# First batch's scores from float32 q and k as loaded, and an earlier, denser weight conversion, in an attention and feed-forward kernel

## The chip, the cores and the metric

The kernel runs on one core of a Trainium2 chip. The metric is the device time of one execution in microseconds (us); lower is better. PE is the matmul engine, DVE the vector engine, ACT the scalar engine, POOL GpSimd, and SP the engine whose queue issues nearly all transfers here.

## What is computed

Talking-heads attention over 4 batches, 12 heads, 448 positions and head size 64, followed by a feed-forward block of 1792 tokens, 768 to 2048 to 768. The weights of the feed-forward block arrive as float64.

```
def _attn_ref(q, k, v, w_pre, w_post):
    scores = np.matmul(q, k.transpose(0, 1, 3, 2)) / np.sqrt(64)
    scores = np.einsum('bhij,hg->bgij', scores, w_pre)
    scores = scores - np.max(scores, axis=-1, keepdims=True)
    attn = np.exp(scores)
    attn = attn / (np.sum(attn, axis=-1, keepdims=True) + 1e-09)
    attn = np.einsum('bhij,hg->bgij', attn, w_post)
    return np.matmul(attn, v)

def _moe_ref(x, w_in, w_out):
    h = x @ w_in
    g = h * (1.0 / (1.0 + np.exp(-1.702 * h)))
    return g @ w_out
```

## The kernel before

**Precision.** Most products run in float16 with each operand split into an upper and a lower half (three products for one). For that, the size of a tensor is found first (`squares`, L122: sums of squares on ACT and DVE; `join`, L136: a product with ones on PE), then a power of two as its scale (`scale`, L139), then the upper half (`upper_part`, L177, on ACT or POOL) and the lower half (`lower_part`, L186, on DVE). The mix with `w_pre` is a float32 product, which PE carries out as two matmul records.

**Attention.** A batch's 448 query rows are cut in 4 chunks of 120 (the last of 88). For each chunk and each of 6 pairs of heads `scores` (L210) makes the products of q and k in two PSUM banks; the two heads of a pair use the two halves of the partitions. `keep_scores` (L227) copies them to SBUF (3 buffers), and `send_scores` (L234) writes them to memory, from where `gather` (L242) reads them back with the rows of 10 queries times 12 heads on the partitions. Each such group is a step; there are 45 a batch and 180 in all. A step's work: `mix` (L252, PE), `peak` (L261, DVE), `expo` (L267, ACT, then a small operation on POOL), `inverse` (L279, DVE: the reciprocal that ends a step), `weigh`, `upper` and `lower` (L283 to L297, POOL and ACT), three steps later `post` (L305, PE), then `keep_upper` on ACT and `keep_lower` on DVE. When a chunk's steps are done, `context` (L337) multiplies with v.

**Weights.** `convert` (L401) turns one slice of one weight matrix (8 slices of w_in, 8 of w_out) from float64 to two float16 halves. A slice has 3 parts. Each part is fetched on SP's queue (L414, 512 KB, 3 buffers), passes through five DVE steps (`magnitude`, `least`, `shift`, `rest`, `sign`, L421 to L441) and a sum of squares on ACT. After the join and the scale each part gets its upper half (`w_upper`, L467, ACT) and its lower half (`w_lower`, L470, DVE), and the slice is stored (L476) in memory. `fetch_w` (L506) loads a converted slice (`wt`) for a unit, that is for one slice and one batch.

**Feed-forward.** A unit's work is cut in 12 quanta of six products: `hidden` (L510, products h at L520) and `project` (L553, products po at L559).

**What sets the order.** Instructions stand in the order in which the Python code issues them. The main loop runs over the steps i. A list of jobs with a first step, an engine, a cost and predecessors is worked off by `run_jobs` (L631) with tokens that `refill` (L601) gives each engine per step. A conversion's jobs get their first step from the call of `convert` (L688): 2, 8, 14 and so on, two matrices a slice, so 12 steps a slice. Once a batch's x is ready (`x_done`), each step may do 2.15 quanta; a unit's quantum is done only if its `wt` load was issued, and `fetch_ahead` (L725) issues the load only when the slice's store was issued at least a step before. What is left after the last step is done densely. Ahead of the loop stand the loads of k and q, their sizes and splits, the first chunk's scores, its first four gathers, and the size of v.

Of the kernel before, what the change touches and what calls it, by code (L numbers as in the profile page):

```python
# [9 lines left out]
F32 = mybir.dt.float32  # L10
# [3 lines left out]
AF = mybir.ActivationFunctionType  # L14
# [24 lines left out]
def attention_then_feed_forward(ctx, tc, q, k, v, w_pre, w_post, w_in, w_out, out):  # L39
# [76 lines left out]
    def load(name, b, i, use, tag="op"):  # L116

        t = st[name, b, i] = flow.tile(SH[name], F32, name=f"{name}{use}{i}_{b}", tag=tag, bufs=THIRDS)
        w = t.shape[1]
        nc.sync.dma_start(out=t, in_=SRC[name][b][:, i * w:(i + 1) * w])  # L120

    def squares(name, b, i, eng, n=1):  # L122
        t = st[name, b, i]
        if ("m" + name, b) not in st:
            st["m" + name, b] = stat.tile([t.shape[0], THIRDS * n], F32, name=f"m{name}_{b}", tag="m" + name)
        x = t.rearrange("p a b -> p (a b)")
        w = x.shape[1] // n
        for y in range(n):
            m = st["m" + name, b][:, i * n + y:i * n + y + 1]
            square_sum(x[:, y * w:(y + 1) * w], m, eng[y % len(eng)])  # L130
# [5 lines left out]
    def join(name, b):  # L136
        add_all(top_of(name, b), st["m" + name, b])

    def scale(name, b):  # L139

        m = top_of(name, b)
        e = stat.tile([128, 1], F32, name=f"e{name}_{b}", tag="e" + name)
        s = stat.tile([128, 1], F32, name=f"s_{name}{b}", tag="s" + name)
        root_bits(e, m)
        nc.vector.reciprocal(s, e)
        nc.vector.tensor_scalar_mul(s, s, 2.0 ** -50)
        nc.vector.tensor_scalar_mul(e, e, 2.0 ** 63)
        st["e" + name, b], st["s" + name, b] = e, s
        if name == "v":
            nc.vector.tensor_scalar(  # L150
                ex[:, b:b + 1], e, e_wp, 2.0 ** -12, op0=ALU.mult, op1=ALU.mult
            )

    def mixing(b):
        c = stat.tile([128, 1], F32, name=f"c_{b}", tag="c")
        nc.vector.tensor_tensor(c, st["eq", b], st["ek", b], op=ALU.mult)
        wa = keep.tile([KG, KG], F32, name=f"wa_{b}", tag="wa", bufs=2)
        nc.vector.tensor_scalar(
            wa, w_mix.rearrange("p i g -> p (i g)"), c[:KG, 0:1], 0.125 * 2.0 ** -26,
            op0=ALU.mult, op1=ALU.mult,  # L160
        )
        st["wa", b] = wa
# [14 lines left out]
    def upper_part(name, b, i, eng):  # L177
        u, _, src, s = pair_of(name, b, i)
        if eng == "A":
            nc.scalar.activation(u, src, AF.Copy, scale=s)  # L180
        elif eng == "D":
            nc.vector.tensor_scalar(u, src, s, 1.0, op0=ALU.mult, op1=ALU.mult)
        else:
            nc.gpsimd.tensor_scalar(u, src, s, 1.0, op0=ALU.mult, op1=ALU.mult)

    def lower_part(name, b, i, eng="D"):  # L186
        u, l, src, s = pair_of(name, b, i)
        nc.vector.scalar_tensor_tensor(l, src, s, u, op0=ALU.mult, op1=ALU.subtract)
# [21 lines left out]
    def scores(b, c, pr, tag=("gen", 3)):  # L210

        i0, n = chunk(b, c)
        two = [bank(f"qk_{b}_{c}_{pr}_{x}", *tag) for x in range(2)]
        done = open_banks[-2:] if tag[0] == "gen" else []
        w = NPAIR // THIRDS
        qp, kp = st["qp", b, pr // w], st["kp", b, pr // w]
        terms = ((0, 0), (0, 1), (1, 0))
        for t, (i, j) in enumerate(terms):
            for x in range(2):
                rs = slice(x * D, (x + 1) * D)  # L220
                nc.tensor.matmul(  # L221
                    two[x][:n, :S], qp[rs, i, pr % w, i0:i0 + n], kp[rs, j, pr % w, :],
                    start=t == 0, stop=t == len(terms) - 1,
                )
        return two, done

    def keep_scores(b, c, pr, two, engs):  # L227
        i0, n = chunk(b, c)
        t = flow.tile([CI, 2, S], F32, name=f"sc_{b}_{c}_{pr}", tag="sc", bufs=3)
        for x in range(2):  # L230
            (nc.scalar.copy if engs[x] == "A" else nc.vector.tensor_copy)(t[:n, x, :], two[x][:n, :S])  # L231
        return t

    def send_scores(b, c, pr, t):  # L234
        n = chunk(b, c)[1]
        nc.sync.dma_start(out=sd[b, c][:, 2 * pr:2 * pr + 2, :], in_=t[:n])
# [164 lines left out]
    def convert(kind, s, first):  # L401
# [5 lines left out]
        def part(a):  # L407
            return slice(a * HW, (a + 1) * HW)
# [52 lines left out]
                    ew[:, s, 2:3], ew[:, s, 0:1], e, 2.0 ** -20, op0=ALU.mult, op1=ALU.mult  # L461
                )

        def w_upper(a):
            if a == 0:
                t["p"] = flow.tile([128, 2, WN], F16, name=f"{nm}_p", tag="wc", bufs=1)
            nc.scalar.activation(t["p"][:, 0, part(a)], t["f", a].bitcast(F32), AF.Copy, scale=t["s"])  # L467

        def w_lower(a):
            nc.vector.scalar_tensor_tensor(  # L470
# [21 lines left out]
        j = job(first, "D", 0.9, scale_w, after=[(j, 0)])  # L492
        low = []
        for a in range(NP):
            up = job(first, "A", 0.65, lambda a=a: w_upper(a), after=[(j, 1)] + [(x, 0) for x in stores[-1:]])
            low.append(job(first, "D", 0.7, lambda a=a: w_lower(a), after=[(up, 1)]))
        parts.extend(low)
        stores.append(job(first, None, 0, store, after=[(x, 1) for x in low]))
# [126 lines left out]
    def job(first, eng, cost, f, after=(), stage=None, urgent=False):  # L625
        j = {"urgent": urgent, "first": first, "eng": eng, "cost": cost, "f": f, "stage": stage,
             "after": [a if isinstance(a, tuple) else (a, 1) for a in after]}
        jobs.append(j)
        return j
# [55 lines left out]
    conv_done = {}  # L685
    for s in range(NS):
        for kind in range(2):
            conv_done[kind, s] = convert(kind, s, 2 + (s * 2 + kind) * 6)  # L688


    quanta = []
# [52 lines left out]


    for i in range(THIRDS):
        load("k", 0, i, "a")
    for i, w in enumerate((w_pre, w_post)):
        nc.scalar.dma_start(out=wrep[:, i, :], in_=w.unsqueeze(0).to_broadcast([GI, H, H]))
    nc.scalar.dma_start(out=wall, in_=w_post.unsqueeze(0).to_broadcast([128, H, H]))  # L750
    nc.vector.memset(ones, 1.0)
    last_pp.append(ps.tile([128, 512], F32, name="sums", tag="av", bufs=1))
    for i in range(THIRDS):
        load("q", 0, i, "a", "w64")
    nc.vector.memset(tops, 0.0)
    nc.scalar.activation(warm, tops[:, 0:1], AF.Exp)
    nc.gpsimd.memset(sel, 1.0)
# [5 lines left out]
        out=sel, in_=sel, pattern=[[H, GI]], compare_op=ALU.is_ge, fill=0.0,  # L763
        base=H - 1, channel_multiplier=-1,
    )
    for name in "kq":
        for i in range(THIRDS):
            squares(name, 0, i, "AD", 2)
        join(name, 0)
        scale(name, 0)  # L770
        for i in range(THIRDS):
            upper_part(name, 0, i, "AGA"[i])
        if name == "k":
            nc.vector.tensor_tensor(
                w_mix,
                wrep[:, 0, :].unsqueeze(1).to_broadcast([KG, GI, H]),
                sel.unsqueeze(2).to_broadcast([KG, GI, H]),
                op=ALU.mult,
            )
        for i in range(THIRDS):  # L780
            lower_part(name, 0, i)
    mixing(0)
    for i in range(THIRDS):
        load("v", 0, i, "a")
        stage_users["op"].append([])
        stage_users["w64"].append([])

    def mixing_pair():
        nc.vector.tensor_reduce(
            rows_w, wall.rearrange("p h g -> p g h"), axis=AX.X, op=ALU.add, apply_absolute_value=True  # L790
        )
        nc.vector.tensor_reduce(top_w, rows_w, axis=AX.X, op=ALU.max)
        nc.vector.tensor_scalar_max(top_w, top_w, 1e-15)
        nc.vector.tensor_single_scalar(
            e_wp.bitcast(I32), top_w.bitcast(I32), 0x7F800000, op=ALU.bitwise_and
        )
        s_wp = stat.tile([128, 1], F32, name="s_wp", tag="swp")
        nc.vector.reciprocal(s_wp, e_wp)
        nc.vector.tensor_scalar_mul(s_wp, s_wp, 16.0)
        nc.vector.tensor_tensor(  # L800
            wp,
            wrep[:, 1, :].unsqueeze(2).to_broadcast([KG, H, GI]),
            sel.unsqueeze(1).to_broadcast([KG, H, GI]),
            op=ALU.mult,
        )
        nc.vector.tensor_scalar_mul(wp1, wp, s_wp[:KG, 0:1])
        nc.vector.scalar_tensor_tensor(
            wp2, wp, s_wp[:KG, 0:1], wp1, op0=ALU.mult, op1=ALU.subtract
        )

    tags = [("gen", 3), ("mx", 2), ("pp", 2)]
    for pr in range(NPAIR):
        two, done = scores(0, 0, pr, tags[pr % 3])
        for x in done:
            x["done"] = True
        t = keep_scores(0, 0, pr, two, "AD")
        send_scores(0, 0, pr, t)
    for i in range(AHEAD):
        gather(i)
    mixing_pair()  # L820
    for i in range(THIRDS):
        squares("v", 0, i, "AD", 2)
    join("v", 0)
    scale("v", 0)
    for i in range(THIRDS):
        up = job(1 + i, {"A": 1.0, "G": 1.6}, 0, lambda eng, i=i: upper_part("v", 0, i, eng))
        stage_users["op"][i] += [up, job(2 + i, "D", 1.05, lambda i=i: lower_part("v", 0, i), after=[up])]


    at_scores = {}  # L830
# [159 lines left out]
```

## Time and profile before

| | |
|---|---|
| median of 3 runs | 1114.95 us (1113.44 to 1118.53) |
| profiled execution: span, first to last instruction | 1113.3 us (the page gives no other time for it) |
| mean granted PE clock, of 2.4 GHz | 0.913 |
| busy: PE, DVE, ACT, POOL | 940.4, 704.9, 659.7, 444.4 us |
| conversion of weights on DVE, 6 lines | 288 instructions |

Busy times add up over stages with different limits, so they are to be read by stretches of the span. The granted clock is given for each stretch as a share of full speed; 0.5 is the lower level, 1.2 GHz, so a mean between 0.5 and 1 is a mixture of the two levels in time. A matmul's records overlap; its busy time is therefore no measure of work.

### The profile page before, as it was taken

Reading aid. Unit: us, or ns where it says so; the run is one execution under the profiler, and the core shown is the slowest. Engines: PE = TensorE matmul, PEld = TensorE weight load, DVE = VectorE, ACT = ScalarE, POOL = GpSimd, SP = SyncE. Lnnn points to the kernel's source line nnn. Section 1 sums busy time; section 2 is a strip of 40 time slices with the busy share of each in tenths; the row PEclk is TensorE's granted clock in tenths of the full one; section 3 lists DMA queues with packets and bytes.
Section 4 is the critical chain, followed back from the end, with each engine's and each line's share of the span. In section 5 each row is a group of like instructions: output and inputs, shape, how many; then the busy total and the mean of one; then the engine's idle time right before and its main releaser. Section 6 shows DMA issues by size and latency. Waiting matters only on the chain.

```text
span 1113.3 us, 21068 instructions
## 1 busy us (share of the span) xinstructions
PE 940.4 (84%) x7768; PEld 548.5 (49%) x7768; DVE 704.9 (63%) x1480; ACT 659.7 (59%) x1479; POOL 444.4 (40%) x601
## 2 busy tenths in 40 slices
PE   2578766688789788768689798899999999999998
PEld 1245444455445454435446464465556566555554
DVE  5688779889867698677664366445655465443333
ACT  4566877787667657656655766756656655332332
POOL 0255446354433355344434346334444445120222
PEclk9776887787898999979699899999999999999999
DMA  6766866766685657645657555755654533134332
GB/s 197 237 212 209 283 229 222 261 210 203 203 262 171 212 187 227 205 138 174 202 155 239 189 170 162 213 148 150 198 170 163 163 116 100 58 129 148 114 114 78
DMA packets 67435, 201.02 MB, mean 181 GB/s; under 512 B 7764, under 2 KB 32468, under 8 KB 67332
## 3 DMA queue, kind: packets, MB, share of 16 engines
q1 hardware_dynamic: 66928, 199.59, 56.2%
q8 instruction: 61, 1.00, 0.4%
q14 instruction: 42, 0.34, 0.1%
q10 hardware_dynamic: 404, 0.09, 0.0%
HBM read 143.02 MB, written 56.62 MB: 179 GB/s over the span
## 4 chain that ended last, share of the span: by engine, by line
PE 53%; DVE 27%; ACT 9%; DMA 5%; issue 4%; POOL 1%; SPq 0%; ACTq 0%; DVEq 0%; POOLq 0%
PE po L559 17%; PE h L520 16%; PE mx L257 7%; PE av L348 4%; DVE p L332 4%; PE qk L221 3%; DVE w_p L470 3%; DVE nm L264 3%; ACT waste L96 2%; DVE w_f L435 2%; PE pp L313 2%; PE pp L315 2%; PE pp L314 2%; DVE w_f L421 2%; DVE w_f L425 2%
## 5 line engine op out<-in xcount | busy, mean ns | idle before, releaser
L559 PE MATMUL po<-g,wt 128*128 128x448 f16 x1152 | 247.7, 359 | 20.8 <-ACT sc L231 9.3
L300 POOL TENSOR_TENSOR a<-w,a 120x448 f16<-120x448 f32 x180 | 202.4, 1124 | 147.9 <-issue 98.6
L520 PE MATMUL h<-x,wt 128*128 128x448 f16 x1152 | 245.4, 358 | 18.4 <-DMA wt<-wd 13.6
L286 POOL TENSOR_SCALAR w<-e,rs 120x448 f32<-120x448 f32 x180 | 119.9, 666 | 327.7 <-DVE rs L281 301.0
L257 PE MATMUL mx<-r,wa 120*120 120x448 f32 x360 | 198.3, 637 | 11.8 <-ACT e L271 9.7
L294 ACT ACTIVATE a<-e,rs 120x448 f16<-120x448 f32 x180 | 121.3, 674 | 138.0 <-DVE rs L281 137.9
L313 PE MATMUL pp<-wp,a 120*112 120x120 f16 x720 | 139.5, 231 | 48.4 <-DVE p L332 47.7
L559 PEld LDWEIGHTS <-wt 128*128 128x128 f16 x1152 | 110.3, 99 | 141.9 <-issue 57.8
L520 PEld LDWEIGHTS <-wt 128*128 128x128 f16 x1152 | 109.8, 99 | 133.5 <-issue 33.3
L315 PE MATMUL pp<-wp,a 120*112 120x120 f16 x720 | 138.9, 230 | 0.0
L314 PE MATMUL pp<-wp,a 120*112 120x120 f16 x720 | 138.7, 230 | 0.0
L541 DVE SCALAR_TENSOR_TENSOR th<-th,h 128x448 f32<-128x448 f32 x64 | 39.6, 619 | 153.1 <-ACT th L538 153.1
L538 ACT ACTIVATE th<-h,ct 128x448 f32<-128x448 f32 x64 | 40.5, 633 | 156.0 <-PE h L520 144.5
L314 PEld LDWEIGHTS <-a 120*112 120x112 f16 x720 | 103.3, 143 | 56.2 <-issue 50.2
L313 PEld LDWEIGHTS <-a 120*112 120x112 f16 x720 | 103.1, 143 | 49.9 <-DVE p L332 26.6
L589 DVE SCALAR_TENSOR_TENSOR acc<-po,ct,acc 128x448 f32<-128x448 f32 x125 | 85.2, 681 | 67.0 <-PE po L559 64.4
L332 DVE TENSOR_TENSOR p<-pp,p 112x480 f16<-112x480 f32 x180 | 116.2, 646 | 6.2 <-ACT p L329 6.2
L271 ACT ACTIVATE e<-mx,nm 120x448 f32<-120x448 f32 x180 | 112.7, 626 | 7.4 <-DVE nm L264 7.2
L231 ACT COPY sc<-qk 120x448 f32<-120x448 f32 (+1 forms) x186 | 89.6, 532 | 41.5 <-PE qk L221 33.7
L264 DVE TENSOR_REDUCE nm<-mx 120x1 f32<-120x448 f32 x180 | 108.7, 604 | 2.4 <-PE mx L257 2.3
L329 ACT CAST p<-pp 112x480 f16<-112x480 f32 x180 | 101.2, 562 | 6.7 <-PE pp L315 6.5
L586 POOL TENSOR_TENSOR acc<-acc,pt 128x448 f32<-128x448 f32 x43 | 52.5, 1223 | 131.4 <-ACT pt L583 130.4
(128 smaller groups left out, 1249.8 us busy)
## 6 DMA issues: line engine op xcount, KB each, us to landing
wt<-wd SPq DMA_DIRECT2D x64, 768.0 KB
r<-sd SPq DMA_DIRECT2D x176, 210.0 KB
sd<-sc SPq DMA_DIRECT2D x72, 420.0 KB
w<-in_moe_w_in_dram SPq DMA_DIRECT2D x24, 512.0 KB
w<-in_moe_w_out_dram SPq DMA_DIRECT2D x24, 512.0 KB
wd<-w_p SPq DMA_DIRECT2D x16, 768.0 KB
sd<-sc SPq DMA_DIRECT2D x24, 308.0 KB
ka<-in_k_dram SPq DMA_DIRECT2D x12, 448.0 KB
```

What stands on the lines that cost most here:

```text
L257: nc.tensor.matmul(mx[:K, :S], st["wa", b][:K, :K], row.pop(("r", i))[:K, :], start=True, stop=True)
L264: nc.vector.tensor_reduce(nm[:K], row["mx", i][:K, :S], axis=AX.X, op=ALU.max, negate=True)
L271: nc.scalar.activation(e[:K], row.pop(("mx", i))[:K, :S], AF.Exp, bias=row.pop(("nm", i))[:K, 0:1], scale=1.0, accum_out=sm[:K, 0:1],)
L286: nc.gpsimd.tensor_scalar(w[:K], e[:K], row["rs", i][:K, 0:1], 1.0, op0=ALU.mult, op1=ALU.mult)
L294: nc.scalar.activation(a1[:K], row.pop(("e", i))[:K], AF.Copy, scale=row.pop(("rs", i))[:K, 0:1])
L300: nc.gpsimd.tensor_tensor(a2[:K], row.pop(("w", i))[:K], row["a1", i][:K], op=ALU.subtract)
L313: nc.tensor.matmul(o, a1[:K, js], wp1[:K, :, :n], start=True, stop=False)
L314: nc.tensor.matmul(o, a1[:K, js], wp2[:K, :, :n], start=False, stop=False)
L315: nc.tensor.matmul(o, a2[:K, js], wp1[:K, :, :n], start=False, stop=True)
L332: nc.vector.tensor_tensor(mixed_to(i, 2), row.pop(("pp", i)), row.pop(("p1", i)), op=ALU.subtract)
L520: nc.tensor.matmul(h, w[:, i, c, fc * 128:(fc + 1) * 128], x[:, j, c, :], start=(n == 0), stop=(n == len(terms) - 1),)
L559: nc.tensor.matmul(po, w[:, j, fc, e * 128:(e + 1) * 128], g[:, i, fc, :], start=(n == 0), stop=(n == len(terms) - 1),)
```

## The change

The first batch's q and k are loaded once into float32 tiles (in the space that its split halves had) and the first batch's scores are float32 products of them, one for each head instead of three. Sizes, scales and splits of the first batch's q and k fall away, and `wa` of the first batch is `w_mix` times 0.125. The conversions' first steps become -6, -1, 4 and so on, ten steps a slice, and `run_jobs` is called with negative steps among the first six score pairs. `w_upper` may go to ACT or to POOL. v's loads and its sizes move from ahead of the loop into the loop's first steps, and `mixing_pair` moves ahead of the first scores.

```diff
+    def load_whole(name, i):
+
+        t = st[name, 0, i] = flow.tile(
+            [128, NPAIR // THIRDS, S], F32, name=f"{name}f{i}_0", tag=f"{name}p{i}"
+        )
+        w = t.shape[1]
+        nc.sync.dma_start(out=t, in_=SRC[name][0][:, i * w:(i + 1) * w])
...
     def mixing(b):
+        wa = keep.tile([KG, KG], F32, name=f"wa_{b}", tag="wa", bufs=2)
+        if b == 0:
+            nc.vector.tensor_scalar_mul(wa, w_mix.rearrange("p i g -> p (i g)"), 0.125)
+            st["wa", b] = wa
+            return
...
+        if b == 0:
+            qf, kf = st["q", 0, pr // w], st["k", 0, pr // w]
+            for x in range(2):
+                rs = slice(x * D, (x + 1) * D)
+                nc.tensor.matmul(
+                    two[x][:n, :S], qf[rs, pr % w, i0:i0 + n], kf[rs, pr % w, :],
+                    start=True, stop=True,
+                )
+            return two, done
...
-        def w_upper(a):
+        def w_upper(a, eng):
...
+            if eng == "A":
+                nc.scalar.activation(u, f, AF.Copy, scale=t["s"])
+            else:
+                nc.gpsimd.tensor_scalar(u, f, t["s"], 1.0, op0=ALU.mult, op1=ALU.mult)
...
-            up = job(first, "A", 0.65, lambda a=a: w_upper(a), after=[(j, 1)] + [(x, 0) for x in stores[-1:]])
+            up = job(first, {"A": 0.7, "G": 0.8}, 0, lambda eng, a=a: w_upper(a, eng), after=[(j, 1)] + [(x, 0) for x in stores[-1:]])
...
-            conv_done[kind, s] = convert(kind, s, 2 + (s * 2 + kind) * 6)
+            conv_done[kind, s] = convert(kind, s, -NPAIR + (s * 2 + kind) * 5)
...
     for i in range(THIRDS):
-        load("k", 0, i, "a")
+        for name in "kq":
+            load_whole(name, i)
...
-    for name in "kq":
-        for i in range(THIRDS):
-            squares(name, 0, i, "AD", 2)
-        join(name, 0)
-        scale(name, 0)
-        for i in range(THIRDS):
-            upper_part(name, 0, i, "AGA"[i])
...
-        for i in range(THIRDS):
-            lower_part(name, 0, i)
...
+    mixing_pair()
     tags = [("gen", 3), ("mx", 2), ("pp", 2)]
     for pr in range(NPAIR):
         two, done = scores(0, 0, pr, tags[pr % 3])
...
         t = keep_scores(0, 0, pr, two, "AD")
+        refill(2.0)
+        run_jobs(pr - NPAIR)
         send_scores(0, 0, pr, t)
...
     for i in range(THIRDS):
-        squares("v", 0, i, "AD", 2)
-    join("v", 0)
-    scale("v", 0)
+        load("v", 0, i, "a")
...
+        sq.append(job(1, {"A": 1.6}, 0, lambda eng, i=i: squares("v", 0, i, eng, 2), urgent=True))
```

What it does to the order is shown at three places. First SP's queue ahead of the loop, before. `va` is a third of v, `sd` takes a pair's scores `sc`, and `r` is a step's gather.

```order
L120 DMA qa2_0_137<-in_q_dram 128x896
L120 DMA va0_0_211<-in_v_dram 112x1024
L120 DMA va1_0_213<-in_v_dram 112x1024
L120 DMA va2_0_215<-in_v_dram 112x1024
L236 DMA sd_0_0_90<-sc_0_0_0_225 120x896
L236 DMA sd_0_0_90<-sc_0_0_1_237 120x896
```

The same place of the changed kernel; `w0_0_64` and `w1_0_64` are the float64 parts of slice 0 of w_in and w_out.

```order
L128 DMA qf2_0_132<-in_q_dram 128x896
L435 DMA w0_0_64_0_164<-in_moe_w_in_dram 128x1024
L435 DMA w0_0_64_1_167<-in_moe_w_in_dram 128x1024
L435 DMA w0_0_64_2_169<-in_moe_w_in_dram 128x1024
L257 DMA sd_0_0_90<-sc_0_0_0_161 120x896
...
L257 DMA sd_0_0_90<-sc_0_0_4_218 120x896
L435 DMA w1_0_64_0_235<-in_moe_w_out_dram 128x1024
L435 DMA w1_0_64_1_238<-in_moe_w_out_dram 128x1024
L435 DMA w1_0_64_2_240<-in_moe_w_out_dram 128x1024
L257 DMA sd_0_0_90<-sc_0_0_5_230 120x896
L268 DMA r_0_243<-sd_0_0_90 120x448
```

Three weight parts now stand ahead of the first scores' store and three ahead of the last; v's loads stand behind the first four gathers.

Second, DVE between the third and the fifth pair's copy in the changed kernel; before, these copies stood next to each other.

```order
L252 COPY sc_0_0_2_184<-qk_0_0_2_1_181 120x448
L442 TENSOR_SCALAR w0_0_f0_187<-w0_0_64_0_164 128x512
...
L456 SCALAR_TENSOR_TENSOR w0_0_f1_193<-w0_0_64_1_167,w0_0_f1_193 128x512
L252 COPY sc_0_0_3_203<-qk_0_0_3_1_200 120x448
L462 SCALAR_TENSOR_TENSOR w0_0_f1_193<-w0_0_64_1_167,w0_0_f1_193 128x512
L442 TENSOR_SCALAR w0_0_f2_209<-w0_0_64_2_169 128x512
L446 TENSOR_SCALAR w0_0_f2_209<-w0_0_f2_209 128x512
L450 TENSOR_SCALAR w0_0_f2_209<-w0_0_f2_209 128x512
L252 COPY sc_0_0_4_218<-qk_0_0_4_1_215 120x448
```

Nine conversion steps now stand between the third and the fourth copy, four between the fourth and the fifth, two ahead of the sixth.

Third, SP at slice 7 of w_in, before; `wd0_7` is the converted slice's store, `wt0_7` its load, and each `r` marks a step.

```order
L476 DMA wd0_7_113<-w0_7_p_7104 128x3072
L236 DMA sd_2_2_100<-sc_2_2_1_7219 120x896
L247 DMA r_105_7270<-sd_2_1_99 120x448
L508 DMA wt0_7_7272<-wd0_7_113 128x3072
```

PE uses this load in the same step: the gather of `r_105` belongs to step 101, and the mix of `r_102` is that step's.

```order
L257 MATMUL mx_102_7274<-r_102_7086,wa_2_4986 120x448
L108 MATMUL pp_97_7252<-mx_1_4296,ones_77 128x8
L520 LDWEIGHTS wt0_7_7272
L520 MATMUL h_7_0_7294<-x_0_1270,wt0_7_7272 128x448
```

In the changed kernel SP has the load in step 87 (the gather of `r_91`), and PE's first product with it stands in step 93, behind the mix of `r_94`.

```order
L501 DMA wd0_7_113<-w0_7_p_5940 128x3072
L257 DMA sd_2_1_99<-sc_2_1_0_6084 120x896
L268 DMA r_91_6171<-sd_2_0_98 120x448
L533 DMA wt0_7_6173<-wd0_7_113 128x3072
```

```order
L278 MATMUL mx_94_6650<-r_94_6441,wa_2_4930 120x448
...
L545 LDWEIGHTS wt0_7_6173
L545 MATMUL h_7_0_6698<-x_0_1231,wt0_7_6173 128x448
```

The load moved from the step of its use to six steps ahead of it. For slice 6 load and product moved from step 91, both, to steps 81 and 88.

## Rows read from the trace of the kernel before

**Rows 1.** Stretches: span; length, busy us (instructions) by engine, PEclk, DMA share, GB/s.

```profile
39.50:137.70 98.20, 73.69 (x561) 43.60 (x558) 77.14 (x161) 72.37 (x171) 49.34 (x72) 0.76 0.75 243
137.70:297.70 160.00, 115.38 (x1055) 72.37 (x1056) 135.48 (x280) 118.83 (x279) 78.25 (x105) 0.79 0.69 224
297.70:480.80 183.10, 154.68 (x1292) 88.36 (x1291) 137.63 (x281) 120.00 (x278) 76.83 (x99) 0.94 0.64 203
480.80:588.70 107.90, 80.82 (x679) 47.74 (x679) 74.35 (x154) 62.51 (x141) 49.04 (x61) 0.83 0.56 173
588.70:944.90 356.20, 340.02 (x3085) 203.25 (x3080) 194.11 (x415) 217.69 (x491) 155.79 (x226) 0.99 0.54 168
```

**Rows 2.** Chain of waits, 484 to 562 us: start us, us, what.

```profile
489.83 7.58 DMA wt<-wd
...
543.69 8.44 DMA wd<-w_p
...
552.15 4.28 DMA wt<-wd
```

**Rows 3.** Timeline, first 62 us: start, us, engine, line, operation, [idle before <-releaser].

```profile
4.28 0.63 DVE L98 SCALAR_TENSOR_TENSOR waste<-ka 128x448 bf16<-128x448 f32 x1 [3.19 <-DMA ka<-in_k_dram]
...
7.33 0.62 DVE L98 SCALAR_TENSOR_TENSOR waste<-ka 128x448 bf16<-128x448 f32 x1 [0.87 <-DMA ka<-in_k_dram]
...
22.95 6.76 SPq L236 DMA_DIRECT2D sd<-sc  x6
...
26.35 0.53 ACT L231 COPY sc<-qk 120x448 f32<-120x448 f32 x1 [3.03 <-DMA sd<-sc]
```

**Rows 4.** Chain of waits ahead of the first mix, 20 to 42 us.

```profile
29.39 4.02 DMA sd<-sc
...
33.47 2.44 DMA r<-sd
...
35.95 3.34 PE mx L257 x4
```

**Rows 5.** Groups by line: line, engine, operation, count | busy us, mean ns | idle before.

```profile
L421 DVE TENSOR_SCALAR w_f<-w 128x512 int32<-128x512 int32 x48 | 30.7, 639 | 0.0
L425 DVE TENSOR_SCALAR w_f<-w_f 128x512 f32<-128x512 f32 x48 | 27.4, 571 | 1.5
L429 DVE TENSOR_SCALAR w_f<-w_f 128x512 int32<-128x512 int32 x48 | 27.7, 577 | 1.5
L435 DVE SCALAR_TENSOR_TENSOR w_f<-w,w_f 128x512 int32<-128x512 int32 x48 | 40.1, 835 | 1.3
L441 DVE SCALAR_TENSOR_TENSOR w_f<-w,w_f 128x512 int32<-128x512 int32 x48 | 43.5, 906 | 1.0
L470 DVE SCALAR_TENSOR_TENSOR w_p<-w_f,w_s,w_p 128x512 f16<-128x512 f32 x48 | 40.9, 900 | 0.0
L467 ACT ACTIVATE w_p<-w_f,w_s 128x512 f16<-128x512 f32 x48 | 31.2, 715 | 0.0
L96 ACT ACTIVATE waste<-va 112x512 bf16<-112x512 f32 x21 | 13.3, 631 | 0.5
```

**Rows 6.** Stretch in the second regime, columns as in Rows 1.

```profile
175.00:200.00 25.00, 18.96 (x159) 10.88 (x157) 24.48 (x44) 17.47 (x40) 13.73 (x18) 0.84 0.75 238
```

**Rows 7.** Timeline of PE, a pair's scores and a mix, at 42 and at 91 us.

```profile
41.89 0.78 PE L221 MATMUL qk<-kp,qp 64*120 64x448 f16 x6
...
42.83 1.01 PE L257 MATMUL mx<-r,wa 120*120 120x448 f32 x2 [0.16 <-ACT e L271]
...
90.79 1.37 PE L221 MATMUL qk<-kp,qp 64*120 64x448 f16 x6
92.09 1.85 PE L257 MATMUL mx<-r,wa 120*120 120x448 f32 x2
```

**Rows 8.** Chain of waits in the dense tail.

```profile
1000.66 3.40 PE h L520 x18
```

**Rows 9.** The tile w_f's instructions: count: duration ns least/median/most, first and last start us.

```profile
L425 DVE TENSOR_SCALAR w_f<-w_f x48: 414/428/1286, 51.2 to 544.1; 128x512 f32<-128x512 f32 x48
```

More of the change, by code (lines that the diff above doesn't have):

```diff
@@ L154, in mixing @@
     def mixing(b):
+        wa = keep.tile([KG, KG], F32, name=f"wa_{b}", tag="wa", bufs=2)
[3 more added lines that the diff above has]
+            return
         c = stat.tile([128, 1], F32, name=f"c_{b}", tag="c")
         nc.vector.tensor_tensor(c, st["eq", b], st["ek", b], op=ALU.mult)
-        wa = keep.tile([KG, KG], F32, name=f"wa_{b}", tag="wa", bufs=2)
         nc.vector.tensor_scalar(
@@ L462, in scale_w @@
                 )
-        def w_upper(a):
+        def w_upper(a, eng):
             if a == 0:
                 t["p"] = flow.tile([128, 2, WN], F16, name=f"{nm}_p", tag="wc", bufs=1)
-            nc.scalar.activation(t["p"][:, 0, part(a)], t["f", a].bitcast(F32), AF.Copy, scale=t["s"])
+            u, f = t["p"][:, 0, part(a)], t["f", a].bitcast(F32)
+            if eng == "A":
+                nc.scalar.activation(u, f, AF.Copy, scale=t["s"])
+            else:
+                nc.gpsimd.tensor_scalar(u, f, t["s"], 1.0, op0=ALU.mult, op1=ALU.mult)
         def w_lower(a):
@@ L752, in attention_then_feed_forward @@
     last_pp.append(ps.tile([128, 512], F32, name="sums", tag="av", bufs=1))
-    for i in range(THIRDS):
-        load("q", 0, i, "a", "w64")
     nc.vector.memset(tops, 0.0)
@@ L765, in attention_then_feed_forward @@
     )
-    for name in "kq":
-        for i in range(THIRDS):
-            squares(name, 0, i, "AD", 2)
-        join(name, 0)
-        scale(name, 0)
-        for i in range(THIRDS):
-            upper_part(name, 0, i, "AGA"[i])
[L773 to L780, printed above, removed]
-            lower_part(name, 0, i)
+    nc.vector.tensor_tensor(
+        w_mix,
+        wrep[:, 0, :].unsqueeze(1).to_broadcast([KG, GI, H]),
+        sel.unsqueeze(2).to_broadcast([KG, GI, H]),
+        op=ALU.mult,
+    )
     mixing(0)
[L783 to L786, printed above, removed]
     def mixing_pair():
@@ L819, in attention_then_feed_forward @@
         gather(i)
-    mixing_pair()
     for i in range(THIRDS):
-        squares("v", 0, i, "AD", 2)
-    join("v", 0)
-    scale("v", 0)
+        load("v", 0, i, "a")
+    sq = []
     for i in range(THIRDS):
-        up = job(1 + i, {"A": 1.0, "G": 1.6}, 0, lambda eng, i=i: upper_part("v", 0, i, eng))
-        stage_users["op"][i] += [up, job(2 + i, "D", 1.05, lambda i=i: lower_part("v", 0, i), after=[up])]
+        stage_users["op"].append([])
+        sq.append(job(1, {"A": 1.6}, 0, lambda eng, i=i: squares("v", 0, i, eng, 2), urgent=True))
+    j = job(1, "D", 0.2, lambda: join("v", 0), after=sq, urgent=True)
+    j = job(1, "D", 0.7, lambda: scale("v", 0), after=[j], urgent=True)
+    for i in range(THIRDS):
+        up = job(1, {"A": 1.0, "G": 1.6}, 0, lambda eng, i=i: upper_part("v", 0, i, eng), after=[j], urgent=True)
+        low = job(1, "D", 1.05, lambda i=i: lower_part("v", 0, i), after=[up], urgent=True)
+        stage_users["op"][i] += [sq[i], up, low]
     at_scores = {}
```

## The prediction

> **What bounds the kernel now.** I read the stretches first, cutting the span at the step reciprocals (L281 on DVE): the rows cover steps 0–23, 24–57, 58–87, 88–105 and 106–177 [rows 1]. The reader is to see three regimes. In the first two stretches DVE is the fullest engine (77.1 of 98.2 us, 135.5 of 160.0) and PE has a granted clock of 0.76 and 0.79: attention waits for vector work, a good part of it the weights' conversion. In the last row PE is busy 340.0 of 356.2 us at 0.99: there, and in the dense tail behind it, PE's own work sets the end. Between them lies a stretch in which nothing is full: steps 88–105 take 107.9 us with PE busy 80.8, DVE 74.4, clock 0.83.
>
> The chain of waits says why [rows 2]. Twice PE stands at the first h product of a slice: at 489.83 for a weight load of 7.58 us, at 543.69 for a store of converted weights of 8.44 us and then, at 552.15, a load of 4.28 us. The planner issues slice 6's and slice 7's load in the very step that uses them; everything that PE has queued behind the product waits too. The conversion is late.
>
> **Head.** Removed: sizes, scales and splits of k and q ahead of the first scores. Now the head waits for transfers. The first pieces of k landed at 4.28, the third at 7.33, so 1.5 us each [rows 3]. Six pieces of k and q then end at 4.28+5x1.5 = 11.8 us. But SP now has three weight loads of 512 KB ahead of the first score store: 3x1.7 more, 16.9 us. In the profile a store's buffer came free 3.4 us after its issue (22.95, copy at 26.35, held by the store) [rows 3]; behind the loads I bound this by 1.2 us (the spacing of later copies is about that) and 3.4: the fourth pair's copy at 18.1 to 20.3 instead of 26.35. From that copy to the first mix took 35.95-26.35 = 9.6 us, of which 4.02 is the last store and 2.44 the gather [rows 4]. To it are added the conversion steps that DVE now has between copies (0.91+0.64+0.57+0.58+0.84+0.91 = 4.45 us [rows 5], where the copies stood 2.3 apart: +2.1) and the three w_out loads ahead of the last store on SP: 5.1 us, of which a part runs beside DVE. First mix between 27.7 (neither counts) and 37.1 (both in full), before 35.95. Nearest row is the store behind a full queue, so I take 35: **-1 us** (ends -8, +1). The sizes of v, which lay in the head, now stand in steps 0–1 on ACT: six squares of 0.63 [rows 5], 3.8 us on a full engine: **+3** (0 to +4).
>
> **Steps 0–23.** By the order, DVE has 86 conversion instructions there instead of 61. Their six kinds average (0.639+0.571+0.577+0.835+0.906+0.900)/6 = 0.74 us [rows 5]: 25x0.74 = 18.5, with v's scale and one more slice's scale some 2 more: DVE goes from 77.1 to 97.6 us. If it fills as between 175 and 200 us (24.5 of 25 [rows 6]; with 5% idle, 102.8), +4.6; if as in steps 24–57 (135.5/160 = 0.85), 115, +17. Steps now carry a conversion nearly each, as at 175–200, but ACT and the exp chain still interleave: **+11**.
>
> **Float32 scores.** A pair of heads was six f16 products in 0.78 us; a float32 mix, the nearest row, is two in 1.01 [rows 7]. If the two heads' halves of the array run side by side, as the f16 ones must (six in 0.78), a pair takes about 1.0, +0.2; if one after the other, 1.8, +1.0. There are 18 pairs in the loop; 0 (PE had 24.5 us idle in steps 0–23) to +18. ACT's copies wait for them directly: I take the near end, **+2**.
>
> **Steps 24–87.** Conversions on DVE 102 instead of 98 and 82 as before: +3 at most. Seventeen uppers of 0.715 us [rows 5] leave ACT: 12 us of an engine busy 74 and 66%; a third of it where ACT is last: **-4** (-12 to +3). PE's quanta per step are the same here.
>
> **Steps 88–105.** Conversion ends in step 91; 3 of its DVE instructions remain of 47. Slice 6's load now stands seven steps ahead of its product and slice 7's six, so the two stops go. One bound: the named waits, 7.58+8.44+4.28 = 20.3 us, less the 48 products more that now stand in this stretch, at 3.40/18 = 0.19 us each [rows 8] 9 us: -11. Other bound: PE's 80.8 us shrunk from clock 0.83 to 0.99 plus 9, at the filling of the next stretch (0.955): (67.7+9)/0.955 = 80, -28. What is late next: batch 1's first h product cannot stand before step 103, since its x is not ready, so slices run out in steps 100–102 and PE is thin there. Between the ends: **-19**.
>
> **Tail.** The same 48 products are missing behind step 105, where PE is the bound: 48x0.19 = **-9**.
>
> Sum: -1+3+11+2-4-19-9 = -17; 1113.3-17 = 1096.3 us. The median of the runs, 1114.95, lies 1.65 above the span: **1098 us**.
>
> **A row that speaks against the move to POOL.** The same 512-element step L425 takes 414 ns at least, 428 at the median and 1286 at most [rows 9]: something stretches it by 0.86 us. 23 of the 48 uppers now run on POOL.
>
> The Trainium skill, SBUF — State Buffer, "Who interferes with whom", says that DVE and GpSimd share one port pair by an exclusive lock, so that the later of two such instructions stands still. By that rule the long L425 are those that met POOL, and each new upper on POOL can stop DVE once; the maximum in the row agrees, the sum above doesn't need it.
>
> **Rivals.**
> 1. The uppers on POOL stop DVE: 22 of the 23 lie in steps 0–87, by the order, and each costs up to 0.86 us on the fullest engine: +19, 1117, no change; half of it, 1107. For it: the maximum of the row. Against: in the median the step is not stretched although POOL was busy half of that time (49.3 of 98.2). This rival is the skill's rule of the paragraph above. Chance 0.18, half of it within 0.5% of no change.
> 2. Slower: the float32 pairs run one after another and at half clock. A mix took 1.85 us in such a stretch and the f16 pair 1.37 [rows 7]; two such products without overlap are 3.7, +2.3 a pair, 18 pairs in the loop +42, and ACT, which copies them, waits with DVE behind it. PE's idle time covers about half: +21 in place of +2 ends the gain (1117), in full 1138. It decides from +1.2 us a pair on the path. For it: clock 0.76 there. Against: PE is not the fullest engine and mix has a step of slack. Chance 0.09.
> 3. The deeper gain: the added DVE work falls into idle time (+5), the head starts 5 earlier, ACT's relief counts for 8, and the late stretch gives 25: -5+1+5+1-8-25-9 = -40, 1075. For it: DVE sat idle 21 us in steps 0–23, mostly while ACT was at exp. Chance 0.18.
> 4. The stops are removed, but the time goes into the wait for batch 1's x at step 103: then only the -11 holds and the sum is -9, 1106: inside the forecast's range, as its upper part.
>
> **How the numbers follow.** A measurement tells about 0.5%, 5.6 us, from no change. The forecast, 1086 to 1109, has 0.55; the rivals as above. Faster by over 0.5% (below 1109.4): 0.55+0.18+0.09 less 0.02 at the edge = 0.80; within: 0.09+0.02 = 0.11; slower: 0.09. The range, for 8 in 10, leaves out the deepest of rival 3 and the outer part of rivals 1 and 2: 1081 to 1114.
>
> **What would show it.** First mix near 35 us. Steps 0–23 some 105 to 115 us long, with DVE above 0.85. A pair's four float32 records in about 1 us at full clock. No wait of PE for wt between steps 88 and 105, that stretch below 95 us, and the dense tail 9 us shorter. I am wrong if the first 24 steps take above 122 us, if PE idles in steps 100–103 as long as it did at the two stops, or if a pair of scores takes over 2 us on the path of ACT's copies.

## The result, and the profile after

The changed kernel takes 1103.51 us (median of 4 runs, 1098.93 to 1107.87), the kernel before 1114.20 in the runs beside it (1112.54 to 1118.53): a ratio of 0.988, 95% interval 0.9838 to 0.9922. The forecast was 1098, with a range of 1081 to 1114: faster, as predicted, by 11 us instead of 17.

The profiled execution is the slowest of the four, 1107.87 us with a span of 1106.1. The view of stretches is cut at the same steps as [rows 1] (0–23, 24–57, 58–87, 88–105, 106–177), with the tail as a sixth row; columns as there.

```profile
42.00:162.20 120.20, 86.09 (x532) 44.89 (x530) 100.79 (x204) 79.69 (x195) 60.70 (x82) 0.74 0.74 242
162.20:322.50 160.30, 116.80 (x1049) 72.38 (x1049) 135.08 (x273) 110.24 (x263) 85.74 (x111) 0.76 0.66 208
322.50:506.60 184.10, 156.82 (x1302) 90.71 (x1301) 141.58 (x298) 118.19 (x275) 81.54 (x106) 0.93 0.65 206
506.60:594.00 87.40, 81.45 (x733) 47.74 (x732) 51.29 (x104) 53.48 (x118) 42.60 (x58) 0.98 0.58 179
594.00:944.40 350.40, 336.71 (x3038) 200.53 (x3038) 192.98 (x416) 212.75 (x484) 153.64 (x221) 0.99 0.52 162
944.40:1106.10 161.70, 157.10 (x1044) 83.43 (x1038) 62.58 (x125) 49.66 (x85) 27.77 (x26) 1.00 0.33 110
```

Against [rows 1] the reader is to see where time came from and went. The head is 2.5 us longer (42.0 against 39.5), steps 0–23 are **22.0** longer (120.2 against 98.2), steps 24–87 1.3 longer. Then steps 88–105 are **20.5** shorter (87.4 against 107.9), steps 106–177 5.8 and the tail 6.7 (before: 1113.3-944.9 = 168.4). Together -7.2, the difference of the two spans. The gain, 33.0 us behind step 87, stands where it was forecast; 24.5 us of it are lost in the head and in steps 0–23.

**The late stretch.** PE's waits between 506.6 and 594 (engine, line, releaser: us in all, times, longest):

```profile
PE po L584 <- DVE th L566: 3.4, 1, 3.4
PE mx L278 <- ACT e L292: 1.8, 2, 1.0
PE pp L334 <- DVE p L353: 0.6, 1, 0.6
```

In the same view of before, between 480.8 and 588.7, the first row was a weight load:

```profile
PE h L520 <- DMA wt<-wd: 13.6, 2, 7.0
```

No load or store of weights is left in PE's waits, and the granted clock of the stretch rose from 0.83 to 0.98.

**The head.** Timeline of the changed kernel (start, us, engine, line, operation, idle before and its releaser):

```profile
14.93 8.98 SPq L257 DMA_DIRECT2D sd<-sc  x5
...
18.89 0.53 ACT L252 COPY sc<-qk 120x448 f32<-120x448 f32 x1 [8.17 <-DMA sd<-sc]
...
23.96 2.23 SPq L435 DMA_DIRECT2D w<-in_moe_w_out_dram  x3
...
26.30 0.37 SPq L257 DMA_DIRECT2D sd<-sc  x1
34.53 1.70 SPq L268 DMA_DIRECT2D r<-sd  x4
...
37.38 3.31 PE L278 MATMUL mx<-r,wa 120*120 120x448 f32 x4 [19.32 <-DMA r<-sd]
...
40.84 1.85 PE L232 MATMUL qk<-kf,qf 64*120 64x448 f32 x4
...
111.88 1.02 PE L232 MATMUL qk<-kf,qf 64*120 64x448 f32 x4
```

The fourth pair's copy stands at 18.89, 7.5 us earlier than in [rows 3]. But the last score store, issued at 26.30 behind three weight loads, lets the gather go only at 34.53: 8.2 us, where the last store of before took 4.02 [rows 4]. Whether that is its place behind the loads in the queue, or the transfer engines that all of them share, is not separated here. The first mix comes at 37.38, later than before (35.95). The last two rows show a pair of float32 heads as four records: 1.85 us, and 1.02 where the clock was full.

### The profile page after: what moved, and what is told of

Its sections match the earlier page's. It is cut to its first block, busy times and chain, and to the rows that moved or that the text cites. A ratio compares the mean times of both kernels' runs of the same rounds, so it can differ in the third digit from the quotient of the medians.

```text
span 1106.1 us, 20863 instructions
## 1 busy us (share of the span) xinstructions
PE 948.5 (86%) x7716; PEld 545.1 (49%) x7716; DVE 699.2 (63%) x1455; ACT 631.3 (57%) x1432; POOL 452.9 (41%) x612
## 4 chain that ended last, share of the span: by engine, by line
PE 56%; DVE 26%; ACT 7%; issue 5%; DMA 4%; POOL 1%; SPq 1%; ACTq 0%; DVEq 0%; POOLq 0%
PE po L584 18%; PE h L545 17%; PE mx L278 7%; PE av L369 4%; DVE w_p L495 3%; DVE p L353 3%; PE qk L242 3%; DVE nm L285 2%; DVE w_f L442 2%; PE pp L334 2%; DVE w_f L456 2%; DVE w_f L446 2%; PE pp L335 2%; PE pp L336 2%; DVE w_f L462 2%
## 5 line engine op out<-in xcount | busy, mean ns | idle before, releaser
L321 POOL TENSOR_TENSOR a<-w,a 120x448 f16<-120x448 f32 x180 | 201.2, 1118 | 153.0 <-issue 85.9
L584 PE MATMUL po<-g,wt 128*128 128x448 f16 x1152 | 250.7, 362 | 11.2 <-DVE th L566 7.2
L307 POOL TENSOR_SCALAR w<-e,rs 120x448 f32<-120x448 f32 x180 | 122.2, 679 | 306.7 <-DVE rs L302 281.8
L278 PE MATMUL mx<-r,wa 120*120 120x448 f32 x360 | 195.3, 628 | 29.0 <-DMA r<-sd 19.3
L334 PE MATMUL pp<-wp,a 120*112 120x120 f16 x720 | 140.0, 232 | 54.9 <-DVE p L353 54.4
L614 DVE SCALAR_TENSOR_TENSOR acc<-po,ct,acc 128x448 f32<-128x448 f32 x137 | 93.3, 682 | 81.1 <-PE po L584 79.1
L335 PEld LDWEIGHTS <-a 120*112 120x112 f16 x720 | 103.4, 144 | 56.7 <-issue 50.6
L334 PEld LDWEIGHTS <-a 120*112 120x112 f16 x720 | 103.1, 143 | 53.9 <-DVE p L353 31.8
L336 PEld LDWEIGHTS <-a 120*112 120x112 f16 x720 | 103.7, 144 | 0.0
```

The lines of the kernel that those rows point to most:

```text
L278: nc.tensor.matmul(mx[:K, :S], st["wa", b][:K, :K], row.pop(("r", i))[:K, :], start=True, stop=True)
L307: nc.gpsimd.tensor_scalar(w[:K], e[:K], row["rs", i][:K, 0:1], 1.0, op0=ALU.mult, op1=ALU.mult)
L321: nc.gpsimd.tensor_tensor(a2[:K], row.pop(("w", i))[:K], row["a1", i][:K], op=ALU.subtract)
L334: nc.tensor.matmul(o, a1[:K, js], wp1[:K, :, :n], start=True, stop=False)
L335: nc.tensor.matmul(o, a1[:K, js], wp2[:K, :, :n], start=False, stop=False)
L336: nc.tensor.matmul(o, a2[:K, js], wp1[:K, :, :n], start=False, stop=True)
```

## Experiments

The loss in the first 24 steps was to be explained. The first theory, called the backlog theory below, was that the moved conversions and the head's transfers cost all of it. Its rivals were rival 1 (an upper half on POOL stops DVE, the lock theory) and rival 2 (float32 pairs on the path). Experiment 1 showed that the choice of POOL for the upper halves costs more than half of the loss; experiments 6 to 10 then asked whether that is what POOL executes, or the order that the planner makes of the choice. Ratios are to the kernel before, timed beside each kernel (medians 1115.3 to 1116.9); brackets are 95% intervals.

**1. All upper halves on ACT.** The changed kernel with

```diff
-            up = job(first, {"A": 0.7, "G": 0.8}, ...
+            up = job(first, {"A": 0.7}, ...
```

> Only the choice of POOL for the weights' upper halves is undone: all 48 on ACT. Backlog theory (the conversions moved into steps 0-23 and the head's transfers cost what the late stretch gives back): the order puts 82 instead of 86 conversion instructions on DVE in steps 0-23, so that stretch stays at 115 to 122 us and the total within 4 us of the changed kernel's 1103.5. Lock theory (POOL's uppers stop DVE): 23 uppers at up to 0.86 us each go, so the run is 8 to 19 us shorter, most of it before step 88, and the long executions (over 1 us) of the steps on w_f become rarer.

1088.7 us, 0.9755 [0.9737, 0.9772]: the choice costs about 15 us, which is the lock theory's range and not the backlog theory's. Steps 0–23 take 108.2:

```profile
41.50:149.70 108.20, 76.18 (x526) 42.89 (x524) 90.75 (x196) 79.41 (x193) 53.30 (x74) 0.78 0.79 255
```

**2. Float32 scores alone.** The changed kernel with the conversions' first steps of before (the choice of POOL stays):

```diff
-            conv_done[kind, s] = convert(kind, s, -NPAIR + (s * 2 + kind) * 5)
+            conv_done[kind, s] = convert(kind, s, 2 + (s * 2 + kind) * 6)
```

> The changed kernel with the conversions' first steps of before (2, 8, 14 and so on): float32 scores, v in the loop and POOL uppers alone. Backlog theory: the stores of the first scores are no longer behind weight loads, so the first mix comes near 25 us instead of 37; steps 0-23 take 98 to 106 us; the two stops of PE for slices 6 and 7 are back (steps 88-105 about 108 us); in all 1100 to 1110. Float32 theory (the pairs themselves lengthen the first steps): steps 0-23 take 112 us or more, the total is over 1115.

1117.1 us, 1.0007 [0.9993, 1.0022]: no change, where the backlog theory had expected 1100 to 1110. The two stops are back (steps 88–105 take 108.4). The first mix comes 10 us earlier, with neither weight loads nor conversion steps in the head:

```profile
27.16 3.25 PE L278 MATMUL mx<-r,wa 120*120 120x448 f32 x4 [11.24 <-DMA r<-sd]
```

The chain of waits shows the last store's issue and its us until the gather goes, in the changed kernel, then here:

```profile
26.30 8.17 DMA sd<-sc
```

```profile
20.12 3.98 DMA sd<-sc
```

So 4.2 of the 10 us are the store's own delay, and 6.2 are its later issue, behind the conversion steps that DVE has between the copies and the issue of the loads.

Against before the head gains 8.8 us and steps 0–23 lose 8.9 (107.1 long). Experiment 8 shows 3.4 of these for the choice; that v's sizes in the loop are the rest is argued, not tried alone.

**3. Early conversion alone.** The kernel before with the changed first steps and nothing else (the reverse of experiment 2's diff).

> The kernel before with the conversions' first steps -6, -1, 4 and so on, nothing else: float16 scores, v ahead of the loop, uppers on ACT; nothing is converted in the head since no jobs run there. Backlog theory: 79 instead of 61 conversion instructions in steps 0-23 make them 10 to 16 us longer than 98; steps 88-105 take 85 to 92 us, and what comes behind is 10 to 13 us shorter; in all 1090 to 1098. Float32 theory: steps 0-23 stay below 104 us and the total falls below 1086.

1094.3 us, 0.9799 [0.9781, 0.9817]. One line gives 22 us, twice what the whole change gave. Steps 0–23 take 107.8 us (+9.6), steps 88–105 91.2 (-16.7). Against experiment 1 the float32 scores, with what comes with them (v in the loop, conversion among the first pairs), are worth 5.6 us.

**4. Every float32 score product twice.** In the changed kernel, the second one into the same bank, with the same result:

```diff
+                for _ in range(2):
                     nc.tensor.matmul(
```

> The changed kernel with each float32 score product carried out twice into the same bank (the second overwrites the first). Float32 theory: 18 pairs in the loop cost 1.0 to 1.8 us more each on the path, so steps 0-33 grow by 18 to 33 us. Backlog theory: DVE is the fullest engine there and PE has slack, so they grow by less than 6 us, and the total stays below 1110.

1106.9 us, 0.9908 [0.9884, 0.9932]: within the changed kernel's interval. A pair now has eight records, 3.35 us at half clock, 1.77 at full:

```profile
104.78 3.35 PE L233 MATMUL qk<-kf,qf 64*120 64x448 f32 x8
112.39 1.77 PE L233 MATMUL qk<-kf,qf 64*120 64x448 f32 x8
```

Steps 0–23 take 120.7 us, 0.5 more. PE has room for these products; rival 2 falls, also by the pair's 1.85 us at half clock, for which it had 3.7.

**5. Experiment 1 with no conversion ahead of the loop.**

```diff
-            conv_done[kind, s] = convert(kind, s, -NPAIR + (s * 2 + kind) * 5)
+            conv_done[kind, s] = convert(kind, s, (s * 2 + kind) * 5)
```

> All uppers on ACT and the conversions' first steps 0, 5, 10 and so on, so that none runs ahead of the loop. Backlog theory: with no weight loads ahead of the first scores' stores the first mix comes near 27 us, as with float32 scores alone, instead of 37; steps 0-23 take 105 to 110 us (78 conversion instructions instead of 82), the late stretch gives back up to 5 us, since slice 7's load stands only two steps ahead of its product: 1078 to 1084. Rival (the head's conversions are work that must be done anyway): the first mix comes earlier, but steps 0-23 grow by as much and the total stays within 3 us of 1088.7.

**1078.9 us**, 0.968 [0.9634, 0.9726], faster than both kernels. The first reciprocal stands at 30.4 instead of 41.5 us; steps 0–23 take 111.3, 3 more than in experiment 1, steps 58–87 2.2 less (175.4), steps 88–105 3.4 more (88.0).

**6 and 7. POOL kept busy, order untouched.** Experiment 1, with the same operation issued on POOL as well for every second upper half, into a tile that nothing reads; then with two memsets of that tile instead, which read nothing:

```diff
+                if (s + kind + a) % 2:
+                    x = flow.tile([128, HW], F16, name=f"{nm}_x{a}", tag="shadow", bufs=1)
+                    nc.gpsimd.tensor_scalar(x, f, t["s"], 1.0, op0=ALU.mult, op1=ALU.mult)
```

> All uppers on ACT, and for 24 of the 48 the same operation done once more on POOL, at the same place, into a tile that nothing reads. Lock theory (a POOL instruction that reads SBUF stops DVE): the run grows by 6 to 15 us over 1088.7 and the median of the steps on w_f behind it grows as in the changed kernel. Dependence theory (DVE's lower half waited for the slower POOL upper): nothing waits for the shadow, so the run stays within 3 us of 1088.7.

> All uppers on ACT, and for 24 of the 48 two memsets of 512 float16 columns on POOL at the same place: POOL is occupied but reads nothing. Lock theory in the form that reading matters: within 3 us of 1088.7. Order theory (POOL is in order, so the next step's weigh and reciprocal input come late): it grows about as much as the shadow by the same operation, in proportion to the memsets' duration.

1090.75 us, 0.9779 [0.9738, 0.9819], and 1089.6, 0.9772 [0.9739, 0.9806]: 1 to 2 us more than experiment 1, with overlapping intervals. So what POOL executes beside DVE in this order is not the 15 us.

**8. The choice alone, in the kernel before.** 19 of the 48 upper halves go to POOL (experiment 1's diff reversed, and `w_upper` with an engine).

> The kernel before with the choice of ACT or POOL for the uppers alone (19 of 48 on POOL by the order). Lock theory: 4 to 14 us longer than before, 1120 to 1130, in the stretches before step 88. If the choice costs only in the changed kernel's crowded first steps: within 4 us of before.

1123.7 us, 1.0078 [1.0047, 1.011]: it costs there too, 3.4 us of it in steps 0–23. Order and engine are not separated in this run; the next two do that in the changed kernel.

**9 and 10. Order and engine apart.** In 9 the planner chooses and charges POOL as in the changed kernel, but every upper half is issued on ACT. In 10 the order is planned with all on ACT, and 24 of 48 are issued on POOL.

```diff
-            if eng == "A":
+            if True:                          # 9
+            if (s + kind + a) % 2 == 0:       # 10, with {"A": 0.7} as the job's engines
```

> The changed kernel's order throughout (the planner still charges POOL for 23 uppers), but every upper is emitted on ACT. Order theory (the choice moves each slice's join and lower halves a step or two earlier, so that a conversion falls into nearly every step): as the changed kernel, 1098 to 1108, steps 0-23 at 116 to 122 us. POOL theory (the 23 uppers' execution on POOL costs the time): as with all uppers on ACT, 1086 to 1093, steps 0-23 near 108 us.

> The order planned with all uppers on ACT, but 24 of the 48 are emitted on POOL. POOL theory: 8 to 15 us longer than the 1088.7 of all uppers on ACT. Order theory: within 4 us of 1088.7.

9: 1103.6 us, 0.9884 [0.9859, 0.9908], the changed kernel's time without one upper half on POOL. 10: 1090.4, 0.9765 [0.9745, 0.9785], experiment 1's time with half of them there. Steps 0–23 of 9, then of 10:

```profile
41.40:161.80 120.40, 84.23 (x532) 44.34 (x530) 98.25 (x204) 84.39 (x203) 52.14 (x74) 0.74 0.73 242
```

```profile
42.00:152.00 110.00, 76.17 (x528) 43.06 (x526) 94.13 (x197) 76.35 (x187) 59.81 (x80) 0.80 0.78 252
```

The 15 us are the order's. Upper halves charged to POOL leave ACT's tokens, and other jobs move: on DVE the joins of the second to the seventh conversion stand one or two steps earlier than in experiment 1, those from the ninth on one to five steps later, with the lower halves behind them. What first shows in the waits is DVE at the join's reduction (`w_n`), for PE's product with ones, over the whole run: the changed kernel, then 9, then experiment 1, then 10.

```profile
DVE w_n L109 <- PE pp L108: 24.8, 10, 4.2
```

```profile
DVE w_n L109 <- PE pp L108: 22.1, 10, 4.2
```

```profile
DVE w_n L109 <- PE pp L108: 1.8, 3, 1.0
```

```profile
DVE w_n L109 <- PE pp L108: 1.5, 2, 1.0
```

**11 and 12. The join's DVE part last in its step.** In the changed kernel, then in experiment 5's kernel, the reduction, root and scale of a weight slice are put off to the end of the step; PE's product and every job's step stay.

```diff
+            late.append(scale_late)
...
             inverse(i)
             spend("D", 0.15)
+        while late:
+            late.pop(0)()
```

> The changed kernel, uppers on ACT or POOL as in it; only the DVE part of a weight slice's join (the reduction, the root and the scale) is issued at the end of its step, behind the step's reciprocal, instead of ahead of the step's post products. PE's product with ones keeps its place, and no job changes its step. In the profile of the changed kernel DVE stood at these joins for 24.8 us (10 times), with everything on ACT in that same order 22.1, with the uppers in ACT's order on POOL 1.5. Theory A, the stop at the join is what the choice's order costs: the wait falls below 5 us, steps 0-23 take 107 to 112 us, the run 1087 to 1094. Theory B, the order costs through its other moves (conversions and lower halves a step earlier), and the wait at the join is only where DVE's idle time shows: steps 0-23 stay at 117 to 122 us and the run at 1100 to 1106. In between, 1095 to 1099: both, by about the share that is gained.

> The version with all uppers on ACT and no conversion ahead of step 0 (1078.9), with the same late join. Its profile had 6.9 us of DVE at these joins, in 6 waits. Theory A: 1 to 5 us faster, 1074 to 1078. Theory B: 1078 to 1081, no change. It is also the control for the edit itself: if a late join costs time by holding the uppers back, this run gets slower than 1081.

11: 1098.0 us, 0.9836 [0.9813, 0.9859], 5.5 faster than the changed kernel. 12: 1084.8, 0.972 [0.9697, 0.9743], 5.9 slower than experiment 5. Both intervals overlap with that of the kernel compared, so both differences are at the edge of the noise. In 11 DVE's row at `w_n` is gone, and steps 0–23 are only 3.5 us shorter, with DVE fuller than before (102.8 of 116.7 us):

```profile
41.10:157.80 116.70, 83.55 (x534) 44.94 (x534) 102.78 (x210) 80.08 (x195) 62.05 (x82) 0.75 0.76 252
```

The edit brings a wait of its own, as 12 shows: the reduction reads a bank of the post products and now frees it only at the end of the step.

```profile
PE pp L339 <- DVE w_n L114: 8.7, 6, 2.3
```

But with the row for `p` beside it PE waits 43.0 us for these banks, against 40.7 in experiment 5, so it explains little of the 5.9. So the stop at the join is at most a part of the order's cost, some 5.5 us net of this edit, and neither theory holds alone.

What the other two thirds consist of was not tried, but the traces show where DVE's work grows. In experiments 1 and 9, both without an upper half on POOL, the first 24 steps hold 82 and 90 conversion steps on DVE, with durations of 54.4 and 64.2 us in all. This is the whole difference in records (196 and 204) and near the 12.2 us by which the stretch grows; DVE as a whole is busy 7.5 us longer, since v's lower halves take less. Half of the 9.8 us are the eight steps more; the other half is that the steps take longer, the lower halves above all. Their rows, in the changed kernel (in 9 the mean is 972), then in experiment 1 (busy us, mean ns, idle before):

```profile
L495 DVE SCALAR_TENSOR_TENSOR w_p<-w_f,w_s,w_p 128x512 f16<-128x512 f32 x15 | 13.8, 970 | 0.0
```

```profile
L495 DVE SCALAR_TENSOR_TENSOR w_p<-w_f,w_s,w_p 128x512 f16<-128x512 f32 x12 | 8.6, 770 | 0.0
```

Steps 24–57 have ten conversion steps fewer for it and give back 4.3 us (158.3 against 162.6 in experiment 1). Steps 58–87 repay nothing: 184.1 us in the changed kernel and in 9, 177.6 and 176.8 in experiments 1 and 10. That more and longer DVE work is the cause, and not only the place where the order's cost shows, is argued.

## Why the prediction was right, and where not

The sign, the place of the gain and the range were right. The terms, against the profiled execution, whose -7.2 us are fewer than the -10.7 of the medians:

| term | predicted | measured |
|---|---|---|
| head | -1 (-8 to +1) | +2.5 |
| steps 0–23, with v's sizes and the float32 pairs | +11+3+2 = +16 | +22.0 |
| steps 24–87 | -4 | +1.3 |
| steps 88–105 | -19 (-28 to -11) | -20.5 |
| behind step 105 | -9 | -12.5 |
| sum | -17 | -7.2 |

**Late stretch and tail: right, for the reason given.** The two stops are gone, PE is nearly full (81.5 of 87.4 us), and by the trace 49 products of h and po more stand in this stretch and 57 fewer behind it, where 48 were forecast. Rival 4, the wait for batch 1's x, did not take the gain.

**Head: too early by 2.4 us.** The prediction took 35, near its far end of 37.1; the first mix came at 37.38, just beyond that end. The last store, with the three loads ahead of it, took 8.2 us from its issue to the gather's, against 4.02 before. Experiments 2 and 5 show what the head would give with neither loads nor conversion steps in it, about 9 us.

**The step that failed** is steps 0–23: "DVE goes from 77.1 to 97.6 us", and "+11", by which DVE would be busy for 0.89 of the stretch. DVE went to 100.8 us and was busy for 0.84 of 120.2, the filling of the term's far end (+17). The work was undercounted by four conversion steps: 86 is the count up to step 23's reciprocal, but the stretch ends at step 24's, and there it is 90 instead of 61. With 29x0.74 the prediction's own sum gives 100.6. The filling was too high even without the choice: it is 0.84 in experiment 1 and 0.83 in experiment 3.

What was priced at nothing is the choice's effect on the planner's order. An upper half that leaves ACT was priced as relief, "a third of it where ACT is last". Steps 24–87 came out at +1.3 instead of -4, and the order cost 15 us in all, 12 of them in steps 0–23. Without the choice the same steps grow by 10.0 us (experiment 1), where +16 was forecast, and by 9.6 with the moved conversion alone (experiment 3): so the +3 for v's sizes and the +2 for the pairs hardly show there.

That the total lay only 5.5 us from the forecast is in part luck. Without the choice it would have been 1088.7, 9 us below the forecast, since the first 24 steps cost less and the stretches from step 88 on gave more than forecast; the choice, priced at nothing, took 15 us the other way.

**Rival 1 had the place and nearly the size, for the wrong reason.** It put +19 or half of it on POOL's upper halves. The measured cost of the choice is 15, but experiment 9 has it with no upper half on POOL, and experiment 10 is without it with half of them there. Stretched DVE steps are real, as the view of the tile `w_f` shows in the kernel before, in the changed kernel, in experiment 1 and in 10 (ns, least/median/most):

```profile
L441 DVE SCALAR_TENSOR_TENSOR w_f<-w,w_f x48: 674/830/1522, 53.6 to 546.8; 128x512 int32<-128x512 int32 x48
```

```profile
L462 DVE SCALAR_TENSOR_TENSOR w_f<-w,w_f x48: 679/693/1520, 17.9 to 494.0; 128x512 int32<-128x512 int32 x48
```

```profile
L462 DVE SCALAR_TENSOR_TENSOR w_f<-w,w_f x48: 681/693/1522, 17.6 to 457.4; 128x512 int32<-128x512 int32 x48
```

```profile
L462 DVE SCALAR_TENSOR_TENSOR w_f<-w,w_f x48: 681/806/1518, 18.2 to 458.8; 128x512 int32<-128x512 int32 x48
```

The longest is the same with and without upper halves on POOL, and the median tells nothing of them: it is 830 in the kernel before, which has none, and 693 in the changed kernel, which has 23. The recorded starts and ends tell more. In the changed kernel 97 of the 288 conversion steps on DVE are over 100 ns longer than the shortest of their line, and all 97 overlap an operation of POOL; of the 114 that overlap none, the longest is 20 ns above the shortest. In the kernel before it is 92 of 92, in experiment 1 77 of 77, in 9 84 of 84. The Trainium skill, SBUF — State Buffer, "Who interferes with whom", has the two engines share a port pair by an exclusive lock; the trace agrees with such a rule in these counts. So rival 1's mechanism is there, but what ran on POOL when such a step began was a step's own `lower` in 52 of the 97, `weigh` in 32 and an upper half in only 8. These stretched steps add 49.4 us to DVE's busy time in the kernel before and 50.2 in the changed kernel. Within one order the upper halves on POOL add 9.5 us to that (experiment 1 to 10) or 5.3 (9 to the changed kernel), and the time grows by 1.7 us and not at all.

**Rival 2 fell** with experiment 4. **Float32 pairs: right in size.** Four records in 1.02 us at full clock is two heads side by side, as two in 1.01 is a mix [rows 7]; at half clock 1.85, as the mix. Its term of +2 was nearer 0, as far as experiment 4 shows it.

**Rival 3's depth was there to be had**, but not in this change: 1075 was given for it, and experiment 5 has 1078.9, by leaving out the choice and the conversion ahead of the loop.

## What to carry to other kernels

Where a planner sets the order by charges, a new choice of engine is first a change of order: look at what moves because of it, and test the order and the engine apart, as experiments 9 and 10 do. A change of several parts is to be split before it is judged: here one line gave 22 us, the float32 scores with what came with them about 6, and the choice of engine took 15 of them back. And work put into a gap ahead of the first results is not free when its loads stand in the queue that the results must pass and its steps between their copies: experiment 5 gained 10 us by taking it out.

## What had not been expected of the hardware

A store behind large loads took longer by more than the loads' issue (2.23 us): with three 512 KB loads ahead, the last score store took 8.2 us from issue to the gather that waits for it, against 4.0 in the kernel before [rows 4]. Doubling the float32 products of a pair (3.35 instead of 1.85 us at half clock) left no mark on the time. And 24 upper halves more on POOL raised the time of DVE's 288 conversion steps from 201.2 to 209.8 us (experiments 1 and 10) and cost at most 2 us of 1089. In these traces it is who begins first that decides: a conversion step that began while one upper half ran, and overlapped nothing else of POOL, took 0.38 to 0.39 us longer than the shortest of its line (5 cases in the changed kernel, 4 in experiment 10), and one that began ahead of a `lower` at most 16 ns (17 cases before, 7 in the changed kernel).
